# Other rows of w4 on each partition, and every seventh column of w3 in a weight load

## The chip, the cores and the metric

The kernel runs on one core of one Trainium2 chip. The metric is the device time of one execution in microseconds (us); the kernel before takes 1078.51 us (median of three runs, 1077.71 to 1079.8).

## The reference, cut to what matters

Two block types are applied twice to eight rows of 448 features: A is attention of one query row against a cache of 4096 keys (16 query heads, 8 cache heads, head size 256), B is a small mixing step and a feed-forward layer. The reference is

```python
x = x + _A_ref(_layernorm(x), K, V, wq, wo)
x = x + _B_ref(_layernorm(x), w1, w2, w3, w4)
# and the same two lines again

# _B_ref, with one row in the sequence (S == 1):
x1 = x + hs                       # hs is zero: every shift takes the row away
h2 = _gelu(_layernorm(x1) @ w3) @ w4      # 448 -> 1792 -> 448
return x1 + h2
```

`w3` is 448 x 1792 and `w4` is 1792 x 448, both bf16. The hidden units, the 1792 columns of `w3` and rows of `w4`, are summed over in the last product, so that they may be numbered in any order as long as both matrices follow the same one. The caches are far larger than all weights: each is 8 x 8 x 4096 x 256 in bf16, 134 MB, and both are read in each of the two attention passes except for what is kept on the chip from the first to the second.

## The kernel before, in words

The work is cut into tasks: a pass (0 or 1), a batch row `b`, and a pair `gp` of cache heads. A task takes four pieces of K and four pieces of V; a piece is 128 partitions x 8192 B, 1 MB. Pieces lie in 15 places of SBUF, the slices of the tile `places`. Twelve of them hold, for a while, pieces of pass 0 that pass 1 of the same batch row reads again (`kept`). A load of two neighbouring K pieces is one DMA of 2 MB (L765), other loads are of 1 MB (L790), and V pieces in `halved` are loaded in two DMAs of 0.5 MB (L793).

All of these loads go out on the queue of SyncE (SP) in the order of the list `loads`; `emit_loads` (L750) is called once per item, and a load into a place waits until the work that read the place is done. The work per piece: K pieces are transposed on VectorE (L803), multiplied with the spread queries on TensorE (L818), exponentiated on ScalarE (L827); V pieces are multiplied with the probabilities on TensorE (`pv`, L871).

The order of the work is written by hand: `items` lists the pieces, and between them the loop at L985 takes steps of generators, among them `chain` (L522). The chain of a batch row is what lies between its two attention passes: the output projection with `wo` (L170 from `add_cols`), the layer norm, the feed-forward layer `mlp` (`mlp_hidden` L397 for `w3`, `out_cols` for `w4`), the projection with `wq`, and the new queries. There are eight chains, one for each batch row. They run in what this document calls the narrow phases: a run of V items in `narrow`, in which the twelve kept places are taken, three places are left to turn over in halves, and the step of a generator stands between the two halves of each V piece (`between` in `pv`, L867) and behind the piece.

In `mlp_hidden` there are 56 products with `w3` for one call: 14 blocks `c` of 128 hidden units, times four parts `fc` of the 448 features. Each product is a matmul with a block of `w3` as its weights, so that a block is loaded into TensorE by its own weight load (LDWEIGHTS, the row PEld of the profile) and a narrow operand passes through it: 32 columns for a single batch row (`wide`, L170), 4 columns for the two calls with four rows (L407). The generator yields after seven blocks, that is after 28 products. `mlp_hidden` is called eight times by chains, once by `rest` for the first four rows of pass 1 (at 942 us, while K and V still stream), and once at the very end (L1136) for the other four, when all attention is done.

`wblk` (L204) gives the 128 columns of a block. For `fc < 3` they are columns 128c to 128c+127 of a part that lies whole on 128 partitions. The fourth part has 64 features only; its columns are folded: the first 896 lie on partitions 0 to 63, the others on 64 to 127, and `wblk` says by its second value which operand (with zeros on the other half) goes with it.

`w4_sb` has the shape 128 x 14 x 448. It is loaded by one DMA on SP's queue (L910), behind `wo` and the three loads of `w3` (L189) and ahead of the second batch of K and V loads:

```python
nc.sync.dma_start(w4_sb[:], B_w4.rearrange("(c p) d -> p c d", p=128))
```

Row 128c + p of `w4` goes to partition p, place c: 14 runs of one row each, 896 B, on each partition, 1792 runs in all. It is read as weights by `out_cols` (L170, L386) and as the moving operand by the last product (L1152).

Of the kernel before, what the change touches and what calls it, by code (L numbers as in the profile page):

```python
# [17 lines left out]
def kernel(  # L18
# [27 lines left out]
    nc = tc.nc  # L46
# [137 lines left out]
    def split_tile(cols, name):  # L184
        return consts.tile([128, 3 * cols + cols // 2], BF16, name=name)

    def load_split(t, src, cols):
        for fc in range(3):
            nc.sync.dma_start(t[:, fc * cols : (fc + 1) * cols], src[fc * 128 : fc * 128 + 128, :])  # L189

    wq_sb = split_tile(HD, "wq_sb")
    w3_sb = split_tile(F, "w3_sb")
    wo_sb = consts.tile([128, NB2, D], BF16, name="wo_sb")
    w4_sb = consts.tile([128, HC, D], BF16, name="w4_sb")
# [8 lines left out]

    def wblk(t, cols, c, fc):  # L204

        if fc < 3:
            return t[:, fc * cols + 128 * c : fc * cols + 128 * c + 128], fc
        half = cols // 2
        if 128 * c < half:
            return t[:, 3 * cols + 128 * c : 3 * cols + 128 * c + 128], 4  # L210
        return t[:, 3 * cols + 128 * c - half : 3 * cols + 128 * c - half + 128], 3
# [111 lines left out]
    def project_q(b0, nb, qT):  # L323

        yield from norm(xT[:, :, b0 : b0 + nb], nb, False)
        q_ps = room_ps("q", nb).rearrange("p (c b) -> p c b", b=nb)
        for j in range(2):
            for h in range(Hq):
                for fc in range(4):
                    w, xi = wblk(wq_sb, HD, 2 * h + j, fc)  # L330
                    if nb == 1:
                        wide(q_ps[:, j * Hq + h, :], w, xbs(1)[:, xi, :], fc == 0, fc == 3)
                        continue
                    nc.tensor.matmul(
                        q_ps[:, j * Hq + h, :],
                        w,
                        xbs(nb)[:, xi, :],
                        start=(fc == 0),
                        stop=(fc == 3),
                    )  # L340
                if h % 8 == 7:
                    yield (3, 0)[j] if h == Hq - 1 else None
        nc.vector.tensor_copy(qT, q_ps)  # L343
        yield
# [52 lines left out]
    def mlp_hidden(b0, nb):  # L397
# [3 lines left out]
        for c in range(HC):  # L401
            for fc in range(4):
                w, xi = wblk(w3_sb, F, c, fc)
                if nb == 1:
                    wide(h_ps[:, c : c + 1], w, xbs(1)[:, xi, :], fc == 0, fc == 3)
                    continue
                nc.tensor.matmul(  # L407
                    h_ps[:, c * nb : c * nb + nb],
                    w,
                    xbs(nb)[:, xi, :],  # L410
                    start=(fc == 0),
                    stop=(fc == 3),
                )
            if c % 7 == 6:
                yield 0 if c == HC - 1 else None
# [491 lines left out]
        A_wo.rearrange("(h p j) d -> p h (j d)", p=128, j=2),  # L907
    )
    load_split(w3_sb, B_w3, F)
    nc.sync.dma_start(w4_sb[:], B_w4.rearrange("(c p) d -> p c d", p=128))  # L910
    for _ in project_q(0, Bn, qT1[:]):
        pass

# [71 lines left out]
    for idx, it in enumerate(items):  # L985
# [7 lines left out]
        n, kv, c = it  # L993
# [5 lines left out]
        p = where[(b, gp), (kv, c)] if kept_now else where[it]  # L999
# [137 lines left out]
    for q in range(4):  # L1137
        for fc in range(4):
            at = min(128 * fc, D - 128)
# [56 lines left out]
```

## Time and profile before

| what | value |
|---|---|
| median of three runs | 1078.51 us (1077.71 to 1079.8) |
| profiled execution | 1078.9 us |
| span of its profile, first to last instruction | 1077.1 us |
| mean granted TensorE clock | 0.663 |
| TensorE matmul, weight load busy | 59%, 37% of the span |
| VectorE, ScalarE busy | 57%, 15% |
| read from HBM | 436.28 MB, 405 GB/s over the span |
| SP's DMA queue | 68880 packets, 435.94 MB, 98.7% of 16 engines' span |

Busy shares are means over the whole span. The profile's page also gives the span in 40 slices, with the busy share of the DMA engines and the GB/s they moved, and a view by windows gives the same for any stretch of time; the chain of waits follows the work that ended last back to the start. A packet is one contiguous run that a DMA engine moves. Tiles whose names differ by a digit are put together: `w_sb` is `w3_sb` and `w4_sb`, and `xb` in the operand tells a `w3` product, `HT_t` or `HTw` a `w4` product.

### The profile page before, as it was taken

Reading aid. Unit: us, or ns where it says so; the run is one execution under the profiler, and the core shown is the slowest. Engines: PE = TensorE matmul, PEld = TensorE weight load, DVE = VectorE, ACT = ScalarE, POOL = GpSimd, SP = SyncE. Lnnn points to the kernel's source line nnn. Section 1 sums busy time; section 2 is a strip of 40 time slices with the busy share of each in tenths; the row PEclk is TensorE's granted clock in tenths of the full one; section 3 lists DMA queues with packets and bytes.
Section 4 is the critical chain, followed back from the end, with each engine's and each line's share of the span. In section 5 each row is a group of like instructions: output and inputs, shape, how many; then the busy total and the mean of one; then the engine's idle time right before and its main releaser. Section 6 shows DMA issues by size and latency. Waiting matters only on the chain.

```text
span 1077.1 us, 29813 instructions
## 1 busy us (share of the span) xinstructions
PE 631.0 (59%) x13292; PEld 399.4 (37%) x13292; DVE 610.7 (57%) x1266; ACT 162.0 (15%) x612; POOL 16.4 (2%) x27
## 2 busy tenths in 40 slices
PE   3244457644765447654586547754775467756775
PEld 2122225422443224432254324532453245433554
DVE  4357841677426872368724773297439743875371
ACT  0001111111111111111111111111111111111110
POOL 0000000000000000000000000000000000000000
PEclk9998568755686556865567656755585567656765
DMA  9999999999999999999999999999999999999994
GB/s 359 394 426 423 426 412 402 424 424 423 403 404 425 426 422 389 417 425 424 420 385 417 424 424 401 397 426 426 409 399 424 424 410 402 425 424 389 409 419 176
DMA packets 69200, 438.22 MB, mean 407 GB/s; under 512 B 7368, under 2 KB 11344, under 8 KB 38736
## 3 DMA queue, kind: packets, MB, share of 16 engines
q1 hardware_dynamic: 68880, 435.94, 98.7%
q8 instruction: 104, 1.70, 0.6%
q10 hardware_dynamic: 192, 0.38, 0.1%
q14 instruction: 24, 0.20, 0.0%
HBM read 436.28 MB, written 0.01 MB: 405 GB/s over the span
## 4 chain that ended last, share of the span: by engine, by line
DMA 64%; PE 18%; DVE 11%; SPq 3%; issue 2%; ACT 2%; POOL 0%; DVEq 0%; ACTq 0%
DMA places<-in_A_v_cache_dram 35%; DMA places<-in_A_k_cache_dram 28%; DVE places L803 7%; PE o L871 6%; PE sc L818 6%; PE misc L170 3%; SPq L189 2%; PE misc L501 1%; SPq L790 1%; ACT p_n L827 1%; DMA wq_sb<-in_A_wq_dram 1%; DVE places L845 1%; DVE store L838 1%; DVE qbd L357 0%; PE misc L854 0%
## 5 line engine op out<-in xcount | busy, mean ns | idle before, releaser
L803 DVE STREAM_TRANSPOSE places<-places 128x512 uint32<-128x512 uint32 (+1 forms) x576 | 457.9, 857 | 127.0 <-DMA places<-in_A_k_cache_dram 125.5
L818 PE MATMUL sc<-places,qbd 128*8 128x256 bf16 (+1 forms) x4896 | 239.8, 343 | 247.8 <-DVE places L803 241.5
L871 PE MATMUL o<-places,ptw 128*8 128x256 bf16 x3968 | 232.4, 360 | 130.7 <-DMA places<-in_A_v_cache_dram 106.1
L818 PEld LDWEIGHTS <-qbd 128*8 128x8 bf16 x4896 | 125.9, 101 | 325.1 <-DVE places L803 147.1
L871 PEld LDWEIGHTS <-ptw 128*8 128x8 bf16 x3968 | 97.9, 99 | 195.5 <-issue 122.1
L827 ACT ACTIVATE p_n<-sc 128x256 bf16<-128x256 f32 x128 | 95.2, 743 | 382.1 <-PE sc L818 382.1
L981 ACT COPY ptw<-psv 128x32 bf16<-128x32 bf16 x248 | 52.6, 227 | 196.4 <-PE o L871 190.5
L861 ACT CAST psv<-misc 128x128 bf16<-128x128 f32 x64 | 17.0, 266 | 237.0 <-PE misc L854 237.0
L465 DVE RECIPROCAL rz<-misc 128x8 f32<-128x8 f32 (+1 forms) x35 | 6.6, 190 | 70.6 <-PE misc L462 70.6
L357 DVE CAST qbd<-misc 32x64 bf16<-32x64 f32 x104 | 22.4, 215 | 29.9 <-PE misc L353 28.9
L170 PEld LDWEIGHTS <-wq_sb 128*128 128x128 bf16 x1024 | 30.0, 101 | 15.2 <-issue 14.7
L170 PE MATMUL misc<-xb,wq_sb 128*128 128x32 bf16 x1024 | 33.5, 184 | 3.6 <-issue 2.9
L501 PE MATMUL misc<-R_t,o_sb 128*128 128x8 f32 (+1 forms) x132 | 26.7, 311 | 13.4 <-ACT o_sb L495 7.1
L170 PEld LDWEIGHTS <-wo_sb 128*128 128x128 bf16 x1024 | 30.1, 102 | 10.9 <-issue 10.7
L170 PE MATMUL misc<-OT,wo_sb 128*128 128x32 bf16 x1024 | 32.7, 185 | 1.9 <-DVE OT L505 1.7
L827 ACT ACTIVATION_READ_ACCUMULATOR p_n<-sc 128x1 f32 x128 | 33.8, 264 | 0.0
L501 PEld LDWEIGHTS misc<-R_t,o_sb 128*128 128x128 f32 x132 | 23.8, 252 | 23.5 <-ACT o_sb L495 13.6
L170 PEld LDWEIGHTS <-w_sb 128*128 128x128 bf16 x896 | 27.3, 103 | 13.8 <-issue 13.2
L343 DVE CAST qT<-misc 128x32 bf16<-128x32 f32 x8 | 1.5, 192 | 50.8 <-PE misc L170 50.8
L269 POOL TENSOR_TENSOR t<-t,nhalf 128x2 f32<-128x2 f32 (+2 forms) x20 | 14.0, 705 | 1048.4 <-DVE t L290 1048.4
L497 DVE MEMSET o<- 128x256 f32 x33 | 9.0, 272 | 34.2 <-PE o L871 31.2
L854 PEld LDWEIGHTS <-p_n 128*128 128x128 bf16 x256 | 11.8, 105 | 31.7 <-issue 20.4
(111 smaller groups left out, 312.3 us busy)
## 6 DMA issues: line engine op xcount, KB each, us to landing
places<-in_A_k_cache_dram SPq DMA_DIRECT2D x65, 2048.0 KB, 19.1
places<-in_A_v_cache_dram SPq DMA_DIRECT2D x107, 1024.0 KB, 21.0
places<-in_A_v_cache_dram SPq DMA_DIRECT2D x202, 512.0 KB, 7.4
places<-in_A_k_cache_dram SPq DMA_DIRECT2D x62, 1024.0 KB, 13.2
places<-in_A_v_cache_dram SPq DMA_DIRECT2D x8, 768.0 KB, 14.3
wo_sb<-in_A_wo_dram SPq DMA_DIRECT2D x1, 3584.0 KB, 27.1
wq_sb<-in_A_wq_dram SPq DMA_DIRECT2D x3, 1024.0 KB, 9.9
w_sb<-in_B_w_dram SPq DMA_DIRECT2D x1, 1568.0 KB
```

The source lines that it names most:

```text
L170: nc.tensor.matmul(bass.AP(out.tensor, out.offset, [out.ap[0], (1, WIDE)]), w, x.to_broadcast([128, WIDE]), start=start, stop=stop, skip_g ...
L189: nc.sync.dma_start(t[:, fc * cols : (fc + 1) * cols], src[fc * 128 : fc * 128 + 128, :])
L269: nc.gpsimd.tensor_tensor(rs[:, k0:k1].rearrange("p n b -> p (n b)"), ve[:, k0:k1].rearrange("p n b -> p (n b)"), nhalf[:].to_broadcast([1 ...
L357: nc.vector.tensor_copy(qbd[32 * a : 32 * a + 32, :, :, a, :], qs.rearrange("p e (f g u h) -> p (e f) u g h", f=2, u=2, h=2)[:, :, u],)
L501: nc.tensor.matmul(ot_ps[:, j], o_sb[:].rearrange("p (i j) -> p j i", j=2)[:, j], R, start=True, stop=True)
L803: nc.vector.transpose(w, w)
L818: nc.tensor.matmul(sc[32 * k : 32 * k + 8, 128 * x : 128 * (x + nx)], qbd[:, ep, gp].rearrange("p a h -> p (a h)"), v, start=(n == 0), sto ...
L827: nc.scalar.activation(p_sb[:, :, :, 2 * u : 2 * u + 2].rearrange("p t i x -> p x t i"), sc[:, 256 * u : 256 * u + 256].rearrange("p (x t ...
L854: nc.tensor.matmul(pt_ps[:, t], p_sb[:, t].rearrange("p i x -> p (i x)"), cols, start=True, stop=True,)
L861: nc.scalar.copy(p_to, pt_ps.rearrange("p t k (a h) -> p a (t k) h", a=4))
L871: nc.tensor.matmul(o_ps[32 * q : 32 * q + 8, :], ptz[:, at : at + 8], v[:, y * Dh : (y + 1) * Dh], start=False, stop=(y >= 12), skip_group ...
L981: nc.scalar.copy(ptw[:, ring_of[it], :, 6:8], psv[slot_of[it[0]]][:, it[2]])
```

## The change

`w4` is laid out anew: hidden unit 896j + 7p + c (j of 2, p of 128, c of 7) goes to partition p, place 7j + c. A partition then takes two runs of seven neighbouring rows, 6272 B each; the DMA has 256 runs in place of 1792, and the same bytes. The hidden units of block 7j + c are now 896j + 7p + c for p = 0 to 127, so that `wblk` takes, for `w3` alone, every seventh column of half j. The halves j are those of the folded fourth part, which is why its two operands are still picked by half. How `w3` lies in SBUF, how it is loaded, and all products with `wq`, `wo` and `w4` are as before; the instructions on every engine stand in the same order with the same shapes and waits, except for the shape of the one DMA (128 x 2 x 3136 elements, before 128 x 14 x 448). The 560 weight loads of `w3` blocks now step 14 B from column to column, before 2 B.

```diff
     def wblk(t, cols, c, fc):
 
+        if t is w3_sb:
+            n = cols // 256
+            at = 3 * cols if fc == 3 else fc * cols + c // n * (cols // 2)
+            return t[:, at + c % n : at + cols // 2 : n], fc if fc < 3 else 4 - c // n
         if fc < 3:
             return t[:, fc * cols + 128 * c : fc * cols + 128 * c + 128], fc
...
     load_split(w3_sb, B_w3, F)
-    nc.sync.dma_start(w4_sb[:], B_w4.rearrange("(c p) d -> p c d", p=128))
+    nc.sync.dma_start(w4_sb[:].rearrange("p (j c) d -> p j c d", j=2), B_w4.rearrange("(j p c) d -> p j c d", j=2, p=128))
```

## The prediction

> **What bounds the kernel now.** I read the page's slices and queue rows first, then the windows, then single lines.
>
> ```profile
> DMA  9999999999999999999999999999999999999994
> GB/s 359 394 426 423 426 412 402 424 424 423 403 404 425 426 422 389 417 425 424 420 385 417 424 424 401 397 426 426 409 399 424 424 410 402 425 424 389 409 419 176
> ...
> q1 hardware_dynamic: 68880, 435.94, 98.7%
> ```
>
> The DMA engines are taken from the second slice almost to the end, so the bytes set the time, and the time of any transfer anywhere in SP's queue counts. But the rate is not even: some slices have 385 to 403 GB/s where others have 424. The dips are the narrow phases. The windows around the `w3` products of the eight chains, in order of the chains (columns: busy us and count of PE, PEld, DVE, ACT, POOL; then granted clock, DMA share, GB/s):
>
> ```profile
> 158.00:166.00 8.00, 5.55 (x124) 3.33 (x120) 2.62 (x15) 0.77 (x4) 0.71 (x1) 0.71 1.03 402
> 287.00:295.00 8.00, 5.96 (x134) 3.71 (x133) 2.05 (x12) 0.77 (x4) 0.70 (x1) 0.61 1.01 385
> 415.00:423.00 8.00, 7.07 (x155) 4.64 (x152) 2.63 (x15) 0.98 (x5) 0.70 (x1) 0.57 0.97 353
> 544.00:552.00 8.00, 6.02 (x141) 3.80 (x137) 2.63 (x15) 0.77 (x4) 0.71 (x1) 0.71 0.99 349
> 663.00:671.00 8.00, 6.43 (x154) 4.10 (x150) 2.63 (x15) 0.77 (x4) 0.70 (x1) 0.71 1.01 390
> 771.00:779.00 8.00, 6.81 (x146) 4.42 (x145) 2.63 (x15) 0.77 (x4) 0.70 (x1) 0.50 1.02 404
> 880.00:888.00 8.00, 5.53 (x131) 3.56 (x128) 2.62 (x15) 0.76 (x4) 0.70 (x1) 0.79 1.02 402
> 989.00:997.00 8.00, 5.47 (x123) 3.38 (x119) 2.62 (x15) 0.77 (x4) 0.70 (x1) 0.68 0.95 338
> ```
>
> Three of them (353, 349, 338) lie far under the 402 to 404 that the same 4096 B packets reach in three others, with a DMA share under 1: there the queue has too little to do. Who holds it up:
>
> ```profile
> SPq L793 <- PE o L871: 114.0, 141, 2.5
> ```
>
> The halves of V are issued when TensorE has finished with a place. In those phases TensorE's steps are part of a loop that paces the DMA. Two of its turns:
>
> ```profile
> 419.09 1.09 PE L170 MATMUL misc<-xb,w_sb 128*128 128x32 bf16 x28
> ...
> 420.64 0.95 PE L170 MATMUL misc<-xb,w_sb 128*128 128x32 bf16 x28
> ...
> 421.52 0.57 PE L871 MATMUL o<-places,ptw 128*8 128x256 bf16 x8
> ```
>
> The 28 `w3` products between two halves take 0.95 us; a half of V, 0.52 MB at 404 GB/s, takes 1.30 us to move. A turn of 28 products and one `pv` half (1.55 us from 419.09 to 420.64) is already longer than the DMA's 1.30. Last, the tail after all loads, which nothing covers:
>
> ```profile
> 1069.22 1.75 PE L407 MATMUL misc<-xb,w_sb 128*128 128x4 bf16 x56 [2.22 <-DVE xb L308]
> ...
> 1071.01 0.22 DVE L425 TENSOR_SCALAR g_t<-misc 128x56 f32<-128x56 f32 x1 [0.65 <-PE misc L407]
> ```
>
> **The change, part by part.**
>
> *The w4 load.* 1.606 MB in runs of 896 B. They move at 38 to 43 us, and there the rate falls:
>
> ```profile
> 16.00:24.00 8.00, 4.86 (x153) 4.20 (x150) 4.30 (x9) 0.00 (x0) 0.00 (x0) 1.00 1.01 421
> 36.00:38.00 2.00, 0.00 (x0) 0.00 (x0) 0.00 (x0) 0.00 (x0) 0.00 (x0) 1.00 1.05 410
> 40.00:43.00 3.00, 0.00 (x0) 0.00 (x0) 0.00 (x0) 0.00 (x0) 0.00 (x0) 1.00 1.12 348
> ```
>
> At 348 GB/s it takes 4.61 us. Runs of 3584 B (`w3`, 36 to 38 us) move at 410, runs of 8192 B (16 to 24 us) at 421. Between them 6272 B takes 3.82 to 3.92 us, which saves 0.7 to 0.8; I take 0.8 because 6272 is nearer to 8192 in time lost per run. As the queue is never empty before the first narrow phase, all of it moves the K loads behind it forward: **-0.8 us**. SP's issue of this DMA is 0.43 us, in a queue that lags the data by about 8 us (issued at 30.1, moving at 38), so a shorter issue is worth nothing. Nothing reads `w4` before 166 us.
>
> *The w3 weight loads.* 560 of them, no instruction more. Before, 28 products in 0.95 us with a last one of 0.19 are (0.95 - 0.19)/27 = 28 ns apart. What a step of 14 B does to a weight load, no row shows; the bounds:
> - Lower end: V blocks as weights at a step of 4 B (L885), 16 products in 0.58 us with a last one of 0.165: (0.58 - 0.165)/15 = 28 ns. So a small step is free, and the 14 B step may be. A gain is excluded, since contiguous columns are never slower in any row.
> - Upper end: fp32 weight loads, which go slower. At L250 two of them take 0.30 us together and one alone at least 0.185, so they start about 0.11 us apart: 82 ns more per product.
> - The row with a like pattern, on another engine: VectorE's reduction L245 reads with a step of 16 B (four rows) and 32 B (eight rows). 128x8 takes 161 ns, 128x32 takes 207, 128x64 takes 261: 1.7 to 1.9 ns an element. The contiguous L242 takes 174 ns for 128x16 and 192 for 128x32, 1.1 ns an element. A far step costs about 1.7 times.
>
> ```profile
> L245 DVE TENSOR_REDUCE t<-t x18: 161/161/207, 158.9 to 1066.2; 128x2 f32<-128x8 f32 x16, 128x8 f32<-128x32 f32 x2
> L242 DVE TENSOR_TENSOR t<-xT,wv x18: 161/164/174, 158.5 to 1065.7; 128x4 f32<-128x4 f32 x16, 128x16 f32<-128x16 f32 x2
> ```
>
> 14 B is nearer to 16 than to 4, so I take 1.7 times: 28 to 48 ns, 20 ns more, 56 x 20 = **1.1 us per call** of `mlp_hidden`. [...]
>
> Where the 1.1 us lands:
> - Tail: L425 waits for the last of 56 products: **+1.1**.
> - Chains in the three starved phases (353, 349, 338 GB/s): each turn is lengthened where TensorE paces the DMA: 3 x 1.1 = **+3.3**.
> - The chains at 385 and 390 GB/s are starved in part; half of it: **+1.1**.
> - The three at 402 to 404: TensorE still waits for V there (its wait on V loads is 106.1 us over 96 waits, 1.1 us each), and 0.55 us more per step fits into it: 0. If that cover is gone, 1.1 each.
> - The call of `rest` at 942 us lies among K pieces, where TensorE waits for VectorE's transposes (241.5 us in all): 0.
>
> Sum: -0.8 + 1.1 + 3.3 + 1.1 = +4.7 us. The profiled execution took 1078.9 us (span 1077.1 and 1.8 around it), 0.4 over the median; against the median: 1078.5 + 4.7 = **1083.2 us**.
>
> **The rivals.**
> 1. *The 14 B step is free; not slower.* For it: the 4 B row at 28 ns. The place is the weight load alone, and it decides while products stay under some 39 ns: 11 ns more is 0.6 us a call, five calls' worth by the sum above (tail, three chains, two halves), 3.1 - 0.8 = 2.3 us. At 28 ns only the `w4` load counts: 1077.7 us. [...]
> 2. *The step costs, but the stream hides it.* TensorE is 59% busy and idles for V within most turns; only the tail pays: -0.8 + 1.1 = +0.3, 1078.8 us. Against it: the three dips.
> 3. *The weight load falls to the fp32 spacing.* 56 x 82 ns = 4.6 us a call, 2.3 us in a turn of 1.3: no wait of 1.1 covers that. Tail 4.6, six of eight chains in full 27.6: 1078.5 - 0.8 + 32.2 = 1109.9 us. [...]
> 4. *More is won than the load.* The three dips lose 8 us x (1 - 347/403) = 1.1 us each; if the phases, starting 0.8 us earlier, fall otherwise and half of the 3.3 comes back: 1078.5 - 0.8 - 1.7 = 1076.0 us. Nothing in the profile says why they should.
>
> **How the numbers follow.** Forecast 0.48, rivals 0.23, 0.10, 0.12, 0.07. The forecast's own range is 1079.9 (tail and one chain: -0.8 + 2.2) to 1091.8 (the load at twice its time, 28 ns more, 1.57 us, on the tail and all eight chains: -0.8 + 14.1). With rivals 1 and 2 the range is 1076.8 (rival 1 less the 0.8 us that the lowest run lies under the median) to 1092, which leaves rivals 3 and 4 out. About 0.2%, 2.2 us, is what a measurement of this kernel can tell from no change: slower 0.44 of the forecast and all of rival 3, 0.56; same 0.23 + 0.10 + 0.04 = 0.37; faster 0.07.
>
> **What would show it.** Right: no dip under 400 GB/s at 38 to 43 us, and the first K transposes after it 0.8 us earlier; 56 `w3` products of the tail in about 2.8 us (before 1.75), the 28 of a step in about 1.5 (0.95) while the `w4` steps stay at 0.95; GB/s at the three dips lower still. Wrong: steps of 0.95 us as before (rival 1), steps of 3 us (rival 3), or long steps with the same GB/s in the windows (rival 2).

## The result and the profile after

The changed kernel takes 1088.38 us (median of six runs) against 1079.4 us before (six runs in all): the ratio is 1.0084 with a 95% interval of 1.0067 to 1.0101, that is 9.0 us slower (7.2 to 10.9). The forecast was 1083.2 us, 4.7 us slower. The direction is as forecast, and so is the place of the loss, the weight loads of `w3`; the loss is 1.9 times as large, and which chains pay it is not as forecast. The execution profiled after took 1090.31 us (span 1088.5), 1.9 above its median, so that single differences between the two profiles are read with at least that much doubt.

The page's slices and queue row after:

```profile
GB/s 354 408 425 426 422 404 395 423 424 422 395 404 426 424 421 389 418 426 422 418 381 419 423 425 371 358 424 426 393 374 426 424 407 393 427 423 395 380 418 170
...
q1 hardware_dynamic: 67344, 435.94, 98.1%
```

1536 packets fewer for the same bytes (1792 runs became 256). The second slice, in which `w4` is loaded, went from 394 to 408 GB/s. The loss lies where the narrow phases are. The deepest fall is in two slices with 401 and 397 GB/s before, which have 371 and 358; they are those of row 4's chain, of which more below.

The window of the `w4` load after (busy columns, granted clock, DMA share, GB/s as before):

```profile
40.00:43.00 3.00, 0.00 (x0) 0.00 (x0) 0.00 (x0) 0.00 (x0) 0.00 (x0) 1.00 1.03 422
```

422 where it was 348: the load itself does what was forecast. The first K transposes behind it start at 47.49 us where they started at 48.13, 0.6 us earlier. The timeline of row 2's chain, TensorE alone, and of the tail:

```profile
419.94 1.69 PE L170 MATMUL misc<-xb,w_sb 128*128 128x32 bf16 x28
421.56 0.60 PE L875 MATMUL o<-places,ptw 128*8 128x256 bf16 x8
422.09 1.68 PE L170 MATMUL misc<-xb,w_sb 128*128 128x32 bf16 x28
...
424.90 0.93 PE L170 MATMUL misc<-HT_t,w_sb 128*128 128x32 bf16 x28 [0.18 <-DVE HT_t L434]
...
1079.26 3.13 PE L411 MATMUL misc<-xb,w_sb 128*128 128x4 bf16 x56 [2.22 <-DVE xb L312]
...
1082.42 0.21 DVE L429 TENSOR_SCALAR g_t<-misc 128x56 f32<-128x56 f32 x1 [2.03 <-PE misc L411]
```

28 products with `w3` take 1.69 us where they took 0.95; the same number with `w4`, contiguous, still takes 0.93. In the tail 56 products take 3.13 us where they took 1.75. The spacing is (3.13 - 0.19)/55 = 53 ns where it was 27 to 28: nearly double, 26 ns more for each, 1.46 us in 56. This is a little high: from the first to the last start of the 56 products, the two traces differ by 1.30 to 1.59 us in the eight chains (1.4 on the mean) and by 1.36 in the tail. The groups by form say the same of the weight load (`w3` and `w4` are one group in the first row, four-row calls with `w3` alone in the second; mean 103 and 106 ns before):

```profile
L170 PEld LDWEIGHTS <-w_sb 128*128 128x128 bf16 x896 | 39.6, 128 | 16.5 <-issue 15.5
L411 PEld LDWEIGHTS <-w_sb 128*128 128x128 bf16 x112 | 6.6, 153 | 4.7 <-issue 4.7
```

One load of `w3` reads as 153 ns busy where it was 106, 47 more, of which 26 are paid in the spacing; loads overlap each other, since 112 of them make 6.6 us of busy time together, 59 ns each.

One sign of being right did not come: the rate in the three dips was to be lower still. The same windows after, moved along with their chains (rows 0, 2, 3 and 7, which had 402, 353, 349 and 338 GB/s):

```profile
158.00:166.00 8.00, 7.27 (x128) 5.20 (x128) 2.23 (x13) 0.44 (x2) 0.70 (x1) 0.50 1.02 362
...
416.00:424.00 8.00, 6.59 (x138) 5.25 (x139) 2.10 (x12) 0.44 (x2) 0.70 (x1) 0.71 0.98 366
545.00:553.00 8.00, 6.22 (x106) 4.45 (x105) 1.75 (x10) 0.22 (x1) 0.70 (x1) 0.59 1.03 405
...
999.00:1007.00 8.00, 6.42 (x130) 5.05 (x130) 2.22 (x13) 0.44 (x2) 0.70 (x1) 0.71 1.01 362
```

The three dips are no deeper, and row 0, which was well fed, has one.

### The profile page after: what moved, and what is told of

Its sections match the earlier page's. It is cut to its first block, busy times and chain, and to the rows that moved or that the text cites. A ratio compares the mean times of both kernels' runs of the same rounds, so it can differ in the third digit from the quotient of the medians.

```text
span 1088.5 us, 29813 instructions
## 1 busy us (share of the span) xinstructions
PE 647.9 (60%) x13292; PEld 415.6 (38%) x13292; DVE 610.6 (56%) x1266; ACT 161.5 (15%) x612; POOL 16.3 (2%) x27
## 4 chain that ended last, share of the span: by engine, by line
DMA 61%; PE 21%; DVE 11%; issue 2%; SPq 2%; ACT 2%; POOL 0%; DVEq 0%; ACTq 0%
DMA places<-in_A_v_cache_dram 35%; DMA places<-in_A_k_cache_dram 24%; PE o L875 7%; DVE places L807 6%; PE sc L822 6%; PE misc L170 5%; SPq L189 2%; DMA w_sb<-in_B_w_dram 1%; ACT p_n L831 1%; DVE store L842 1%; PE misc L505 1%; DVE places L849 1%; DMA wq_sb<-in_A_wq_dram 1%; PE misc L858 1%; POOL t L273 0%
## 5 line engine op out<-in xcount | busy, mean ns | idle before, releaser
L170 PEld LDWEIGHTS <-w_sb 128*128 128x128 bf16 x896 | 39.6, 128 | 16.5 <-issue 15.5
L170 PEld LDWEIGHTS <-wo_sb 128*128 128x128 bf16 x1024 | 29.7, 101 | 11.0 <-issue 10.9
L170 PE MATMUL misc<-xb,w_sb 128*128 128x32 bf16 x448 | 26.9, 214 | 3.0 <-DVE xb L302 3.0
```

The costliest lines, as they stand in the source:

```text
L170: nc.tensor.matmul(bass.AP(out.tensor, out.offset, [out.ap[0], (1, WIDE)]), w, x.to_broadcast([128, WIDE]), start=start, stop=stop, skip_g ...
```

## The experiments

The theory after the result: the `w4` load gains about 1 us, and TensorE's 1.46 us for each call of `mlp_hidden` is paid in the tail and, through the turns of the narrow phases, by the chains. Each group of runs was compared with runs of the kernel before on the same chip.

### The two halves of the change, each alone

The load alone, with the weight loads contiguous:

```diff
-    nc.sync.dma_start(w4_sb[:], B_w4.rearrange("(c p) d -> p c d", p=128))
+    nc.sync.dma_start(w4_sb[:].rearrange("p (j c) d -> p j c d", j=2), B_w4.rearrange("(j p c) d -> p j c d", j=2, p=128))
```

> The w4 load in runs of 6272 B alone; w3 is read contiguously as before, so the hidden units of the two matrices no longer belong together and the output is another. Theory (the load wins, the weight loads lose): 0.6 to 0.8 us faster than before, 1077.7 against 1078.5; the first K transposes after the w4 transfer 0.6 us earlier, products with w3 at 28 ns. Rival A (the new load itself, or the shift of all later work by 0.6 us, makes the narrow phases worse): slower than before by 2 us or more.

Measured: 1077.84 us, ratio 0.9989 (0.9980 to 0.9998), 1.2 us faster (0.2 to 2.2); its first K transposes start at 47.24 us, 0.9 earlier than before. Rival A falls. The step alone is the changed kernel with the old DMA:

```diff
-    nc.sync.dma_start(w4_sb[:].rearrange("p (j c) d -> p j c d", j=2), B_w4.rearrange("(j p c) d -> p j c d", j=2, p=128))
+    nc.sync.dma_start(w4_sb[:], B_w4.rearrange("(c p) d -> p c d", p=128))
```

> The 14 B step of the w3 weight loads alone; w4 is loaded in runs of 896 B as before (output another, for the same reason). Theory: slower than before by what the changed kernel loses plus the 0.7 us that the load no longer gives, 1.5 us in the tail and about 8 in the chains: 1088 to 1090. Rival A: most of the loss is gone, under 1083.

Measured: 1089.14 us, ratio 1.0086 (1.0067 to 1.0105), 9.3 us slower. The whole loss sits in the weight loads.

### TensorE's time or a disturbance in SBUF

With the new load and contiguous `w3`, each product made twice:

```diff
-                if nb == 1:
-                    wide(h_ps[:, c : c + 1], w, xbs(1)[:, xi, :], fc == 0, fc == 3)
-                    continue
...
+                for k in range(2):
+                    if nb == 1:
+                        wide(h_ps[:, c : c + 1], w, xbs(1)[:, xi, :], fc + k == 0, fc + k == 4)
+                        continue
...
```

> New w4 load, contiguous w3, and each product with w3 made twice (the sums double, output another): the same TensorE time as the 14 B step, 112 products at 27 ns for 56 at 53, with no far step. Theory (it is TensorE's time in the turns and in the tail that costs): as slow as the changed kernel, 1087 to 1090. Rival B (the far reads themselves disturb others in SBUF, the DMA's writes above all): only the tail's 1.5 us and little of the chains, under 1083.

Measured: 1090.62 us, ratio 1.0107 (1.0087 to 1.0127), 11.5 us slower, a little more than was expected. A step of it in the timeline, 56 products in the time of the changed kernel's 28:

```profile
419.61 1.71 PE L170 MATMUL misc<-xb,w_sb 128*128 128x32 bf16 x56
421.25 0.60 PE L872 MATMUL o<-places,ptw 128*8 128x256 bf16 x8
421.78 1.73 PE L170 MATMUL misc<-xb,w_sb 128*128 128x32 bf16 x56
```

With no far step at all the kernel is at least as slow, so TensorE's time is enough to explain the loss, and Rival B is not needed. (The run also makes 560 weight loads and products more than the changed kernel, so that a small part of Rival B is not excluded by it.)

### What a step costs

Another step for each call, in elements of 2 B:

```diff
                 w, xi = wblk(w3_sb, F, c, fc)
+                s = (2, 3, 4, 5, 6, 8, 10, 16)[b0] if nb == 1 else (7 if b0 else 14)
+                at = min(fc, 2) * F + c
+                w = w3_sb[:, at : at + 127 * s + 1 : s]
```

> Each call of the hidden layer reads w3 with another step: the chains of rows 0 to 7 take columns 4, 6, 8, 10, 12, 16, 20 and 32 B apart, the call of the first four rows 28 B, the tail 14 B (output another). Read: spacing of the products. [...] Theory 2 (a threshold between two steps): 28 ns up to some step and 53 behind it, nothing between. Theory 3 (it grows with the step): more than 53 ns at 28 and 32 B.

The run was executed once. The timeline, one group of 28 for each chain (steps of 4, 6, 8, 10, 12, 16, 20, 32 B in this order), then the tail's 56 (14 B):

```profile
164.18 0.97 PE L170 MATMUL misc<-xb,w_sb 128*128 128x32 bf16 x28
...
293.05 0.98 PE L170 MATMUL misc<-xb,w_sb 128*128 128x32 bf16 x28
...
421.80 1.12 PE L170 MATMUL misc<-xb,w_sb 128*128 128x32 bf16 x28
...
551.11 1.30 PE L170 MATMUL misc<-xb,w_sb 128*128 128x32 bf16 x28
...
669.00 1.50 PE L170 MATMUL misc<-xb,w_sb 128*128 128x32 bf16 x28
...
778.32 1.88 PE L170 MATMUL misc<-xb,w_sb 128*128 128x32 bf16 x28
...
890.63 1.83 PE L170 MATMUL misc<-xb,w_sb 128*128 128x32 bf16 x28
...
1001.20 1.91 PE L170 MATMUL misc<-xb,w_sb 128*128 128x32 bf16 x28
...
1076.39 3.14 PE L410 MATMUL misc<-xb,w_sb 128*128 128x4 bf16 x56 [2.22 <-DVE xb L308]
```

The medians of the spacing from start to start: 28 ns at 4 and 6 B, 33 at 8, 40 at 10, 47 at 12, 53 at 14, 60 at 16, then 58 at 20, 60 at 28 and 62 at 32 B. It is flat up to 6 B, rises by 5 to 7 ns for every 2 B up to 16, and is about flat behind. A jump between two steps (Theory 2) is out: 33, 40 and 47 ns lie between. Theory 3 named more than 53 ns at 28 and 32 B, and 60 and 62 came, but the growth ends at 16 B. From 8 to 16 B the spacing grows by 27 ns, 3.4 for each byte of the step. A spacing of 6 ns and 3.4 for each byte, but never under 28, gives 40, 47 and 54 at 10, 12 and 14 B, as measured within 1 ns. That is a line laid through these spacings; why a step costs was not shown.

### Who pays: the tail, and which chains

The changed kernel with the step kept in some calls only; `far` is set for each call from its rows. The diff is that of chains 0, 5 and 6; the other runs have (2, 3, 7), (4,) or (1,) in the same place, the tail's run has `nb > 1`, and the last has `nb == 1 and b0 != 4`:

```diff
     def wblk(t, cols, c, fc):
 
-        if t is w3_sb:
+        if t is w3_sb and far[0]:
...
+                far[0] = nb == 1 and b0 in (0, 5, 6)
                 w, xi = wblk(w3_sb, F, c, fc)
```

> New w4 load; the 14 B step only in the two calls with four rows (the tail, and the call among K pieces at 942 us), contiguous w3 in the eight chains (output another). Theory (the tail pays its 26 ns x 56 = 1.5 us in full, the call at 942 us nothing, the chains the other 8 to 9): 1.5 - 1.0 = 0.5 us slower than before, which is no difference that can be told. Rival C (the end decides, the chains are covered): 8 us slower or more.

> New w4 load; the 14 B step only in the chains of rows 0, 5 and 6, those in whose windows the DMA engines kept 402 to 404 GB/s before (output another). The prediction's reading (TensorE's wait for V covers 0.7 us more in a step there): only the load's gain is left, 1.0 us faster than before. Theory now (every chain pays, as each turn is longer than the DMA's 1.3 us whatever the window's rate was): 3 x 1.1 to 1.5 - 1.0 = 2.3 to 3.5 us slower than before.

> The same with the chains of rows 2, 3 and 7, in whose windows the rate was 338 to 353 GB/s before. Both readings: 3 x 1.1 to 1.5 - 1.0 = 2.3 to 3.5 us slower than before; it is the measure for the run with rows 0, 5 and 6, which under the prediction's reading would be some 4 us faster than this one and under the theory now equal to it.

> New w4 load; the 14 B step only in the chain of row 4 (output another). In the profiles with the step in all chains, and with doubled products, this chain alone moves all later work back by 4 to 7 us, and the others by 0 to 3 each. Theory D (the loss is uneven: in this chain the queue runs empty, and what TensorE adds comes back several times over): 4 - 1 = 3 us slower than before. Theory E (every chain pays its own 1.5 us, and the jump at row 4 is what came together in three profiles): 1.5 - 1.0 = 0.5 us slower, no difference that can be told.

> The same with the chain of row 1 alone. Theory D: 0 to 1 - 1 = 0 or a little faster than before. Theory E: 0.5 us slower, the same as with row 4.

> The 14 B step in all calls but the chain of row 4 (this includes the tail's call). Theory D: 4 us or more of the 9 to 10 come back, 4 to 6 us slower than before. Theory E: 1.5 us come back, 8 us slower than before. A third reading (the delays of several chains add to more than their sum, since each begins with the queue emptier): 7 us slower or more, with both single chains near zero.

The last run leaves the step out of all calls with four rows too, the tail's among them, which its expectation wrongly counts in: its step is in seven chains and nowhere else, so that its expectations of 4 to 6 us (Theory D) and 8 us (Theory E) come down by the tail's 1.5.

| step kept in | ratio to before (95%) | us to before | less the load's -1.2 |
|---|---|---|---|
| nothing (load alone) | 0.9989 (0.9980 to 0.9998) | -1.2 | 0 |
| tail and the call at 942 us | 0.9999 (0.9988 to 1.0009) | -0.1 | 1.1 |
| chains 0, 5, 6 | 1.0017 (1.0001 to 1.0033) | 1.8 | 3.0 |
| chains 2, 3, 7 | 1.0001 (0.9989 to 1.0012) | 0.1 | 1.3 |
| chain 4 | 1.0017 (1.0004 to 1.0030) | 1.8 | 3.0 |
| chain 1 | 0.9999 (0.9982 to 1.0015) | -0.1 | 1.1 |
| all chains but 4, no tail | 1.0044 (1.0029 to 1.0059) | 4.7 | 5.9 |
| all | 1.0084 (1.0067 to 1.0101) | 9.0 | 10.2 |

Each entry of the last column is uncertain by 1.5 to 2 us, the two intervals put together. The parts add up to 1.1 + 3.0 + 1.3 + 3.0 + 1.1 = 9.5 against 10.2, and the chains without 4 to 3.0 + 1.3 + 1.1 = 5.4 against 5.9. The doubt of the load's gain enters such a sum with every part, so that the first agreement is good to some 5 us only. The third reading of the last expectation asked for 7 us or more with both single chains near zero; 4.7 (3.1 to 6.4) came. As it stands it falls, but a smaller loss that only several chains together bring is not excluded.

- Tail: as far as 1.1 with its 1.5 us of doubt tells, the 1.46 us that it takes longer.
- Chains: about 1.1 us each on the mean (8.4 by the parts, 9.1 by the whole less the tail), against 1.46 us of TensorE's time. Chains 0, 5 and 6, in whose windows the rate had been 402 to 404 GB/s, pay no less than 2, 3 and 7 with 338 to 353: both runs were made on one chip, and the medians stand at 1081.73 and 1080.59 us where the prediction's reading had the first some 4 us faster. So the reading that V's waits cover them falls. The other half of it is not borne out either: chains 2, 3 and 7 were expected 2.3 to 3.5 us slower than before and came out 0.1 slower (1.3 faster to 1.3 slower), less than the 4.4 us of TensorE's time in three chains even at the upper end. Why they pay so little stays open.
- Chain 4: 3.0 alone, 10.2 - 5.9 - 1.1 = 3.2 (with about 3 of doubt) by leaving it out; twice its own TensorE time, but the interval of the 3.0 (1.3 to 4.7) holds 1.46 too. Whether it pays more than its own time (Theory D) or not (Theory E) stays open. The jump at row 4 in single profiles does not decide it. From the first `w3` product of row 4 to that of row 5, all work falls further behind the profile before by 4.4 us in the changed kernel, 3.0 with the step alone and 1.8 with doubled products, not the 4 to 7 of the expectation; by 3.9 in the run with chain 1 only, where 28 products of chain 4 take 0.95 us; and by 1.3 in the run with chain 4 only.

### Why the windows misled

These are the windows of the load-alone run, with products at 28 ns as in the kernel before, at the same eight places as in the prediction:

```profile
158.00:166.00 8.00, 6.49 (x140) 4.09 (x139) 2.63 (x15) 0.98 (x5) 0.70 (x1) 0.61 1.03 400
287.00:295.00 8.00, 6.58 (x157) 4.30 (x150) 2.57 (x15) 0.98 (x5) 0.70 (x1) 0.78 0.96 356
415.00:423.00 8.00, 4.79 (x98) 2.93 (x98) 2.10 (x13) 0.70 (x4) 0.70 (x1) 0.62 0.97 335
544.00:552.00 8.00, 5.43 (x120) 3.29 (x120) 2.27 (x13) 0.94 (x5) 0.70 (x1) 0.66 1.01 396
663.00:671.00 8.00, 6.42 (x159) 4.43 (x160) 2.30 (x14) 0.98 (x5) 0.70 (x1) 0.79 1.01 403
771.00:779.00 8.00, 6.01 (x154) 4.35 (x151) 2.62 (x15) 0.76 (x4) 0.70 (x1) 0.73 1.00 375
880.00:888.00 8.00, 6.83 (x146) 4.29 (x140) 2.45 (x14) 0.54 (x3) 0.70 (x1) 0.50 1.01 381
989.00:997.00 8.00, 6.83 (x153) 4.48 (x149) 2.37 (x14) 0.44 (x2) 0.69 (x1) 0.50 1.01 386
```

Rows 3 and 7 had 349 and 338 GB/s before and have 396 and 386 here; rows 1 and 5 had 385 and 404 and have 356 and 375. The two kernels differ by one load at 38 to 43 us alone. So where the queue runs low does not look like a property of the chain; that it does run low in some narrow phase or other is common to both. A window of 8 us of one execution does not say which chain has something to spare.

Nor do TensorE's waits for V in the profile before tell the two groups apart. In 26 us that take in the chain's `w3` products, in row 0 (160 to 186 us; 402 GB/s) and in row 7 (990 to 1016 us; 338 GB/s):

```profile
PE o L871 <- DMA places<-in_A_v_cache_dram: 6.5, 10, 0.9
```

```profile
PE o L871 <- DMA places<-in_A_v_cache_dram: 5.1, 7, 1.0
```

The first number is the sum in us. Rows 5 and 6, well fed too, have 2.0 and 5.8; rows 2 and 3, starved, have 6.0 and 5.7. In the changed kernel's profile those of rows 0, 5 and 6 are 3.2, 0.6 and 4.3 us, in the load-alone run's 6.5, 2.6 and 2.1, so that these waits too differ from one execution to another.

### A version with the gain and without the loss

The new `w4` load, and `w3` put in the new order once, so that its blocks are contiguous again. It needs no second copy of `w3` in SBUF: ScalarE turns seven runs of 896 columns through two banks of PSUM that are free until the first pieces are stored there; reads and writes stand at alternate items 20 to 33, before the first chain:

```diff
+    def turn_w3(k):
+
+        half = w3_sb[:, k // 2 * (F // 2) : (k // 2 + 1) * (F // 2)]
+        far = half.rearrange("p (q c) -> p c q", q=128)
+        parts = ((store[2], 0, 4), (store[3], 4, 7))
+        for t, c0, c1 in parts * (k % 2 == 0):
+            nc.scalar.copy(t[:, 0 : 128 * (c1 - c0)].rearrange("p (c q) -> p c q", q=128), far[:, c0:c1])
+        for t, c0, c1 in parts * (k % 2):
+            nc.scalar.copy(half[:, 128 * c0 : 128 * c1], t[:, 0 : 128 * (c1 - c0)])
...
+        if 20 <= idx < 34:
+            turn_w3(idx - 20)
```

> The new w4 load with the columns of w3 put in the new order once: ScalarE copies each run of 896 columns of w3 (seven of them, early in the stream, before the first call) through two banks of PSUM back into its place, every seventh column first, and all weight loads read contiguously as before. Output as the reference's. Theory: 28 products in 0.95 us again, the copies lie in ScalarE's idle time (15% busy) while the DMA engines keep their rate, so that the load's gain alone is left: 1.0 us faster than before, 1077.8. Rival: the copies hold up exponentials and the places they free, 0 or slower.

Measured: 1079.53 us against 1080.11 for before on that chip, ratio 0.9988 (0.9976 to 1.0000): 1.3 us faster, as the load alone is, but with an interval that ends at no change. The groups of the copies, into PSUM and back:

```profile
L989 ACT CAST store<-w_sb 128x512 f32<-128x512 bf16 (+1 forms) x14 | 11.6, 869 | 0.0
L991 ACT CAST w_sb<-store 128x512 bf16<-128x512 f32 (+1 forms) x14 | 6.9, 537 | 0.2
```

They take 18.5 us of ScalarE, between 80 and 121 us, while the loads go on. It is 10 us better than the change as made, and at the edge of what can be told from the kernel before.

## Why the prediction was right, and where its sum was off

- *The w4 load, -0.8 us.* Right: it moves at 422 GB/s where 348 was, the first K transposes come 0.6 to 0.9 us earlier, and alone it gives 1.2 (0.2 to 2.2).
- *The weight load, 28 to 48 ns by VectorE's ratio of 1.7.* Right in kind, too small: 53 ns. The row chosen was the right one of the three, and 14 B was read rightly as nearer to 16 (53 ns, against 60 at 16 B and 28 at 4); with TensorE's load at a step of 16 B and more the products are 2.1 to 2.2 times as far apart as at 4 B (58 to 62 ns for 28), VectorE's reduction takes 1.7 times as long (1.7 to 1.9 ns an element for 1.1). That the two come so near is in part luck: another engine and another operation were compared, and the 128x8 form of L245, a single row's, is not a stepped read, since its four elements lie side by side. With the contiguous 1.1 ns an element for it, the stepped forms come to 1.7 ns and the ratio to 1.5. The larger size makes 1.46 for 1.1 us a call and, over the forecast's five calls' worth, 1.8 us of the 4.3 missing (1.46 x 5 - 5.5).
- *The tail, +1.1.* Right within what could be measured; by TensorE's row +1.38 (3.13 less 1.75).
- *Starved chains pay in full, +3.3; those at 385 to 390 GB/s half, +1.1; those at 402 to 404 nothing.* This is the step that failed. Chains 2, 3 and 7 pay 1.3, chains 1 and 4 pay 4.1, chains 0, 5 and 6 pay 3.0: 8.4 in all where 4.4 was forecast. The price of a chain does not follow the rate in its window. The cover named for the last three was a mean over 96 waits of the whole kernel (106.1 us), and with the step in these three chains alone the time was lost all the same. The prediction had named this case (if that cover is gone, 1.1 each): 4.7 + 3.3 = 8.0 us, inside the measured 7.2 to 10.9. One likely reason was already in the prediction's own lines and not drawn out: a turn with 28 products takes longer than the 1.30 us of the DMA, 1.41 to 1.55 us in seven of the eight chains (1.28 in row 4), so that TensorE lags while its chain lasts, and the waits it has before and after are those of an empty queue. After, the turn takes 2.13 to 2.29 us in all eight. That this is the reason was not tested. That the total still lies inside the forecast's own range owes something to errors that went opposite ways: the starved chains pay less than was forecast, the others more.
- *The call at 942 us, 0.* Not measured apart from the tail; the two profiles show half of it covered: behind its first 28 products TensorE's wait for a transpose falls from 1.03 to 0.39 us, while the last 28 take 1.66 us where they took 0.91, with no wait behind them.
- *Rivals.* 1 (free step) falls with the doubled spacing. 2 (hidden in the stream) falls with 8 to 9 us in the chains; the dips that were held against it are, as shown, no good witness. 3 (the spacing of fp32 loads) falls: even a step of 32 B gives 62 ns, not 110. 4 (more is won than the load) falls: it asked for 2.5 us, and the load alone gives 1.2 (0.2 to 2.2).

What happened lies midway between the forecast's middle (4.7 us slower) and its own upper bound, a doubled load paid by the tail and all eight chains (13.3): 9.0 came. In kind it is the upper bound that describes it: 9 calls at 1.46 less 1.2 are 11.9 us, with some of it not paid.

## What to carry to other kernels

A layout that makes a DMA's runs longer by interleaving rows moves the step into whatever reads the matching operand, so price that read for every time it is done: here 560 weight loads were charged for one load of 4.6 us. Steps of up to 6 B between bf16 columns cost a weight load nothing here (28 ns from product to product), 14 B nearly doubled the spacing (53 ns); if the long runs are wanted, put the other operand in order once, on an engine that is idle (ScalarE here, 15% busy, 18.5 us for the copies). And before a part of the stream is called covered because its window looked well fed, look at the same window in a second execution, at the waits there and not at their mean over the kernel, or at whether the turn of the loop there is shorter than the transfer that it paces.

## What was not expected of the hardware

In row 4's chain TensorE pauses between the 20th and the 21st of 32 products with `wq`, with nothing to wait for in the profile, in both kernels. The lines from the profile before, from after, and from the run with chain 1 alone, one fence each:

```profile
681.24 0.50 PE L170 MATMUL misc<-xb,wq_sb 128*128 128x32 bf16 x12 [1.29 <-issue]
```

```profile
686.45 0.52 PE L170 MATMUL misc<-xb,wq_sb 128*128 128x32 bf16 x12 [2.74 <-issue]
```

```profile
686.29 0.51 PE L170 MATMUL misc<-xb,wq_sb 128*128 128x32 bf16 x12 [3.54 <-issue]
```

In each of these traces a 16 KB packet of the instruction queue lands 1.4 to 1.6 us before the pause ends (at 679.9, 684.9 and 684.9 us), and in the two with the long pause the packet starts at 684.0 us where it started at 678.9 in the trace before. Eleven of the thirteen traces have a pause at this same product, of 0.96 to 3.54 us, and in all eleven it ends 1.3 to 1.6 us after such a packet lands; the other two, with doubled products and with `w3` turned, have none over 0.9 us at this product. That TensorE waits for its instructions there, and that a late fetch made part of the jump at row 4 in some profiles, fits this, but no run was made to show it. Nor do the profiles tell how much of a median it makes: the one with the 3.54 us is of an execution of 1086.09 us, 6.3 above the median of its run.
